# A forward and backward pass of four attention layers on one core: spread weight loads, halved score tiles, 66 identity products and a few moved steps

## The chip, the cores and the metric

The kernel runs on one core of one Trainium2 chip. The metric is the device time of one execution in microseconds (us). Three runs of the kernel before gave 2131.43, 2122.83 and 2129.14, so the median is 2129.14. Engines are named as in the profile: PE is TensorE (matrix products; PEld its weight loads), DVE is VectorE, ACT is ScalarE, POOL is GpSimd, and SP is SyncE, whose queue (SPq) issues every DMA of this kernel in program order.

## The reference

A sequence of 2048 rows of width 640 passes through four residual layers with two sets of weights, A, B, A, B. Each layer normalises its input, projects it to 32 heads of 20 columns, applies attention, projects back and adds the input. Layers 0 and 2 (A) are linear attention, layers 1 and 3 (B) are softmax attention in a window of 256 rows. The outputs are the last `x`, and the gradients for the input and the four weight matrices.

```python
def _A_ref(x, wqkv, wo):                     # H = 32, Dh = 20
    q, k, v = heads(x @ wqkv)
    phi = lambda t: jnp.where(t > 0, t + 1, jnp.exp(t)) + 1e-6
    pq, pk = phi(q), phi(k)
    kv, z = einsum("bhsd,bhse->bhde", pk, v), einsum("bhsd->bhd", pk)
    o = einsum("bhqd,bhde->bhqe", pq, kv) / (einsum("bhqd,bhd->bhq", pq, z)[..., None] + 1e-6)
    return merge(o) @ wo
def _B_ref(x, wqkv, wo):                     # causal, window W = 256
    p = softmax(where(mask, q @ k.T * Dh ** -0.5, -1e9))
    return merge(p @ v) @ wo
for f, w in ((_A_ref, A), (_B_ref, B), (_A_ref, A), (_B_ref, B)):
    x = x + f(_layernorm(x), *w)
out, vjp = jax.vjp(...);  grads = vjp(grad_out)
```

## The kernel before

The rows are cut into 16 tiles of 128. The kernel is one long program whose order on each engine is written by hand: every step of every tile is a closure with a place (a slot number), `forward` and `core` sort them by place, and the engines' queues are filled in that order. The table `PLACES` holds the offsets. Nothing reorders them afterwards; an engine does its own list in order and waits where an operand or a buffer is not ready. DMAs go to SP either at once (`dma`) or, through `put` (L153), so many slots later.

**The forward** has three overlapping stretches. `plan_first` (L650) does layer 0's projections, six slots per tile: products with `WA`, feature maps on ACT and DVE (L670 to L672), whose result tile `pqk` has two buffers and is stored to HBM by SP. The weights of layer 1, `WB`, are loaded in this stretch, at the places `ld` (L49, L365). From slot 118 on, `plan_front` (L523) finishes layer 0 for a tile and begins layer 1: quotients `o` on DVE (L559 to L561), transposes on PE with a copy back (`flip`, L220), products with `WoA` and `WB`, and two DMA transposes `T<-s` that bring queries and keys into the form the scores need. `plan_scores` (L445) computes the scores of a tile in six visits of four blocks: 16 products into one PSUM tile `sT` of four banks (one buffer, L462), one exponential of 128x2048 on ACT (L469), masks on POOL (L477, L480), and products with the values (`ops`, L286). Layers 2 and 3 repeat this from slot 302 on. `warm` (L233) issues products of the identity with itself into a PSUM tile from the ring `st.ps`; nobody reads them. The lists `fw` and `fn` (L64, L65) give places and counts of such products in the forward; all counts are 0.

**The backward** of a B layer is `core` (L1433): visits of eight blocks, three or four blocks in each of two halves. A visit computes scores `s` and, three visits later, `dp`; ACT makes `e` (L811), POOL masks it (L826, L830), DVE multiplies `ds` (L815), PE or a DMA transpose turns it into `dsT` (L818, L837), and three visits after that `acc` adds the gradients (L854). The operands of a quarter of a chunk, the slabs, are loaded by `core_loads` (L1392): `slabT` and `slabqT` for scores, `slabks` and `slabqs` (two buffers) for `acc`. `plan_before` (L909) prepares the next chunk: loads of `gb` and `ob` (one buffer), PE transposes of `gb`, products, and `fold` and `split` on POOL. The backward of an A layer is `plan_linear` (L1117); the last step of a tile, two additions of 128x640 (L1220, L1229), is on POOL, for the last tile of layer 2 on DVE. In `passes` (L1502) the first three visits of layer 1's core are issued at the offsets `B1_` (L77) among the last steps of layer 2's backward. The weight gradients `wg` come last.

Of the kernel before, what the change touches and what calls it, by code (L numbers as in the profile page):

```python
# [10 lines left out]
ACT = mybir.ActivationFunctionType  # L11
# [3 lines left out]
F32 = mybir.dt.float32  # L15
P = 128
D = 640
H = 32
DH = 20
HP = 32  # L20
T = 2048
TT = T // P
DT = D // P
SPM = (True, True, False, True, True, False)
G = H // 4
# [9 lines left out]
CW = D // 2  # L35
# [6 lines left out]
PLACES = dict(  # L42
    f1=[0.2, 1.1, 3.6, 8.1, 10.1, 11.8, 13.6, 14.1, 14.5, 14.6, 14.5, 16.1],
    f2=[-30.6, -24.5, -23.3, -20.4, -18.2, -17.7, -16.5, -14.9, -13.5, -7.7, -5.9, -5.8, -4.8, -3.3, -1.7, 10.6, 11.7, 12.6, 14.3, 16.6, 22.8, 23.8, 23.9, 25.1, 26.9, 26.7],
    f3=[-36, -31.4, -27.1, -25.2, -23.8, -23.8, -19.6, -17.6, -17.1, -14.1, -9.6, -8.1, -6.3, -5.3, -5, -4, -1.2, 11.7, 12.2, 13.7],
    s1=[0, 1.33, 2.67, 3.8, 5.83, 6.97, 1.4, 1.43, 2.77, 6, 6.63, 8.17, 2.7, 4.8, 5.7, 5.8, 7.4, 8.5, 9.6, 10],
    s3=[-0.3, 0.83, 2.77, 4, 5.43, 6.67, 0.2, 2.8, 4.67, 4.8, 5.58, 6.72, 3.9, 5.3, 6, 6.1, 7.2, 8.1, 9.7, 9.9],
    wt=[100, 101.9, 104, 104, 108, 110, 112.5, 115.2, 118, 118, 120.5, 122, 124, 126, 128.5, 279.3, 280.7, 280.7, 282, 282.8, 283.4, 283.7, 284.8, 285.9, 287.7, 288, 288.2, 288.2, 289.1, 291.6, 291.8, 292.5, 292.8, 293, 293, 293, 293.2, 295.1, 296.4, 296.4],
    ld=[39.8, 61, 63, 69.7, 82.8],  # L49
    sp=[2.6, 1.1, -2.9, -3.4, 0.6, -3.8, 0.1, 0.4, 2, 1.8, 1.1, 0.8, 3, 1, 0.9, 0.5, 1.3, 1.1, 1, 1, 1.5],  # L50
    ms=[1, -0.2, 20, 31.2, 39.5],
    bf=[1.6, 4.2, 7.7, 10, 17.8, 7.7, 9.2, 10, 14, 28.4],
# [8 lines left out]
    ws1=[8, 8, 8, 8, 8, 8, 8, 8, 8, 8, 8, 8],  # L61
    wp=[1.5, 3.5, 7.2, 9.2, 12, 15, 18, 21],
    wn=[0, 0, 0, 0, 0, 0, 0, 0],
    fw=[100, 120, 136, 268, 284, 298, 420, 428],  # L64
    fn=[0, 0, 0, 0, 0, 0, 0, 0],  # L65
    l2=[-10.1, -1.3, 0.6, 1.1, 1.9, 3, 4.6, 6.4, 7, 7.3, 5, 8, 8.3, 10.2, 11.6, 14, 15.2, 15.3, 16, 16.2, 18.7, -2.5, 3.9],
    n1=[9.7, 0.5, 3.3, 3.6, 5.3, 9, 3, 4.7, 5.4, 5.6, 24],
    th=[0, 2, 1, 4, 1, 0, 0, 0, 0, 3, 0, 1, 0, 0, 0, 4, 8, 5, 0, 1, 2, 2, 1, 1],
# [5 lines left out]


TAILV = (0, 0, 1, 2, 3, 4, 5)
B1_ = (4, 5, 6)  # L77
BEF, BEF1 = -26, 14


# [11 lines left out]
class Kern:  # L92
# [209 lines left out]
    def forward(self, st):  # L302
# [8 lines left out]
        nc = self.nc  # L311
# [21 lines left out]
        WA, WoB = vp.tile([P, DT, QT], BF, name="WA"), wo.tile([P, DT, D], BF, name="WoB")  # L333
        WB, WoA = wp.tile([P, DT, QT], BF, name="WB"), wp.tile([P, DT, D], BF, name="WoA")

        def cols(w, kind, c):
            self.dma(w[:, :, c * D:(c + 1) * D], self.W[kind][:, c * D:(c + 1) * D].rearrange("(k p) n -> p k n", p=P))

        def square(w, kind):
            self.dma(w, self.Wo[kind].rearrange("(k p) n -> p k n", p=P))  # L340
# [14 lines left out]
        plan = []  # L355
        for t in range(TT):
# [5 lines left out]
        plan += [(a, lambda c=c: cols(WA, "A", c)) for a, c in zip((0.5, 1.5, 2.5), (1, 2, 0))]  # L362
        plan += [(a + (1.2 * k if a > 1 else 0), lambda R=R, k=k: pads(R, k)) for a, R in zip(PLACES["ms"], st.ring) for k in range(5)]
        plan += [(0.2, lambda: self.warm(36, st.ps.tile([P, 8, P], BF, name="warm", tag="m")))]
        plan += list(zip(PLACES["ld"], (lambda: square(WoA, "A"), lambda: cols(WB, "B", 1), lambda: cols(WB, "B", 0),  # L365
                                        lambda: cols(WB, "B", 2), lambda: square(WoB, "B"))))

        plan += [(a, lambda n=n: self.warm(n, st.ps.tile([P, 8, P], BF, name="warm", tag="m"))) for a, n in zip(PLACES["fw"], PLACES["fn"]) if n]
        stage = {"j": -1}
# [17 lines left out]
        turns = [(w, d_, j, n - 1) for w, d_, n in ((WA, self.WT["A"], NF), (WoB, self.WoT["B"], DT), (WB, self.WT["B"], NF), (WoA, self.WoT["A"], DT)) for j in range(n)]  # L387
        plan += [(a, lambda x=x, i=i: turn(*x, i % 4 != 3)) for i, (a, x) in enumerate(zip(PLACES["wt"], turns))]

        def scores():  # L390
            first.close()
            st.ps = ps
            st.pSs = ExitStack()
            st.pS = self.pool(st.pSs, "pS", 1, bass.MemoryType.PSUM, "right")
        c1, c3 = 118, B1 + 144
        plan += [(c1, lambda: self.close_outer(self.mz[0], [m[0:KB, 0:3 * KA] for m in st.M])), (c1 + 9, lambda: self.turn_outer(st, self.mz[0], self.mzT[0])),
                 (B1 - 1, scores), (c3, lambda: (self.close_outer(self.mz[2]), self.counted(st.outs, 2 * TT))),
                 (c3 + 9, lambda: self.turn_outer(st, self.mz[2], self.mzT[2]))]

        class B3_:  # L400
# [44 lines left out]
    def plan_scores(self, st, l, t, X):  # L445
        nc = self.nc
        nb = min(t, 2) + 1
        k0 = t - nb + 1
        blocks = [(g, i) for g in range(G) for i in range(nb)]
        nv = len(blocks) // 4  # L450
        home = {}

        def ring(k):
            R = st.ring[k % len(st.ring)]
            assert R["of"] == (l, k)
            return R

        def visit(v):
            if v == 0:
                X[t]["ob"] = st.fa.tile([P, D], BF, name="ob")  # L460
            qT = ring(t)["T"]
            s = st.pS.tile([P, 4, 512], F32, name="sT")  # L462
            for j, (g, i) in enumerate(blocks[4 * v:4 * v + 4]):
                for hh in range(4):
                    r0 = HP * hh
                    self.mm(s[:, hh, j * P:(j + 1) * P], ring(k0 + i)["T"][r0:r0 + HP, 1, g, :], qT[r0:r0 + HP, 0, g, :],
                            True, True, (r0, 0))
            e = st.fpe.tile([P, 4, 4 * P], BF, name="eT", tag="e")
            nc.scalar.activation(e, s, ACT.Exp)  # L469
            for j, b in enumerate(blocks[4 * v:4 * v + 4]):  # L470
                home[b] = e[:, :, j * P:(j + 1) * P]

        def masks(v):
            for g, i in blocks[4 * v:4 * v + 4]:
                e = home[g, i]
                if i == nb - 1:
                    nc.gpsimd.affine_select(out=e, in_=e, compare_op=ALU.is_ge, fill=0.0, base=0,  # L477
                                            pattern=[[0, 4], [1, P]], channel_multiplier=-1)
                elif nb == 3 and i == 0:
                    nc.gpsimd.affine_select(out=e, in_=e, compare_op=ALU.is_ge, fill=0.0, base=-1,  # L480
                                            pattern=[[0, 4], [-1, P]], channel_multiplier=1)

        def values(g):
            X[t]["pv"] = g
            self.b_pv(st, l, t, g, [home[g, i] for i in range(nb)], nb, [ring(k0 + i) for i in range(nb)], X[t]["ob"])
        if nb < 3:
            pv = [g + 2.99 for g in range(G)]
            sc = [(G * v / nv, G * v / nv + 0.9) for v in range(nv)]
        else:
            a = PLACES["s1" if l == 1 else "s3"]  # L490
            sc, pv = list(zip(a[0:6], a[6:12])), a[12:20]
        plan = []
        for v in range(nv):
            plan += [(sc[v][0], lambda v=v: visit(v)), (sc[v][1], lambda v=v: masks(v))]
        return plan + [(pv[g], lambda g=g: values(g)) for g in range(G)]
# [270 lines left out]
        return ("FPA", "PFA", "PAF", "FAP", "AFP", "APF")[PLACES["fo"][n % 24] if 48 <= n < 192 else 0]  # L766

    V0 = 8
    WARM = (8, 5)
    TAIL = 5  # L770

# [345 lines left out]
    def plan_linear(self, st, lp, l, t, X, WT, g_out):  # L1117

        nc = self.nc
        eng = nc.vector if l == 2 and t == TT - 1 else nc.gpsimd  # L1120
        sv = self.sv[l]
        i = t % 2
        x = {}
# [268 lines left out]
    def core_loads(self, l, c, qr, B):  # L1392
        sv = self.sv[l]
        t0 = 2 * c
        w0 = max(t0 - 2, 0)
        S = {}
        if qr == 0 and c == 0:
            B.kept = []
        new = dict(c=c, qr=qr, T=B.keep.tile([P, 2, 2, 2, P], BF, name="slabT", bufs=7))
        old = B.kept[-4] if c else None  # L1400
        B.kept.append(new)

        def part(kind, dst, k, a, n):
            if k == "T":
                out, src = dst.rearrange("p a t g f -> p (a t g f)"), sv[k][c][:, qr, a:a + n].rearrange("p a t f -> p (a t f)")
            else:
                out, src = dst.rearrange("p a t g f -> p t a (g f)"), sv[k][t0:t0 + 2, :, a:a + n, qr * 2 * P:(qr + 1) * 2 * P].rearrange("t p a f -> p t a f")
            self.put(kind if c or qr else 0, out, src, now=c + qr == 0)
        q = B.slab.tile([P, 1, 2, 2, P], BF, name="slabqT", bufs=2)
        part(16, new["T"], "T", 1, 2)  # L1410
        part(17, q, "T", 0, 1)
        S["qT"] = q[:, 0]

        def late():
            new["s"] = B.keep.tile([P, 1, 2, 2, P], BF, name="slabks", bufs=6)
            q = B.slab.tile([P, 1, 2, 2, P], BF, name="slabqs", bufs=2)
            part(18, new["s"], "s", 1, 1)
            part(19, q, "s", 0, 1)
            S["qs"] = q[:, 0]
        S["late"] = late  # L1420

        def window(k, a):
            def at(kk, n):
                i = w0 + kk - t0
                return new[k][:, a, i:i + n] if i >= 0 else old[k][:, a, 2 + i:2 + i + n]
            return at
        S["kT"], S["vT"], S["ks"] = window("T", 0), window("T", 1), window("s", 0)
        for nm in ("ds", "dT"):
            S[nm] = [B.ring[(t0 + i) % 4][nm] for i in range(2)]
        S["ring"] = [(B.ring[(t0 + i) % 4], (l, t0 + i)) for i in range(2)]  # L1430
        return S

    def core(self, st, l, g_out, B, hooks):  # L1433
# [4 lines left out]
        plan = []  # L1438
        dq = {}
        for c in range(1, NC):  # L1440
            for a, *f in B.next if c == 1 else self.plan_before(st, l, c, B):
                if c == 1:
                    a = self.V0 / 0.75 + a * (1 - self.V0 / 24) if a < 32 else a
                plan.append((32 * (c - 1) + a, *f))
# [286 lines left out]
```

## Time and profile before

| | us |
|---|---|
| median of three runs | 2129.14 |
| lowest and highest | 2122.83, 2131.43 |
| the profiled execution | 2130.39 |
| its span, first to last instruction | 2128.6 |
| DVE busy in it | 1387.4 |
| ACT busy in it | 1301.5 |
| POOL busy in it | 1014.2 |

The profile is of one execution, and all rows quoted here are from it. A row of the timeline has the start, the duration, the engine, the source line, the tiles (output, then inputs) and the count of merged instructions; in brackets behind it stands how long the engine sat idle before, and what ended that. A row of the table by windows has the stretch, its length, then for PE, PEld, DVE, ACT and POOL the busy time with the number of instructions, the granted clock of PE (1.00 is full speed), the share of the DMA engines and GB/s. The row of a group has the busy time, the mean duration in ns, and the idle time before with its releasers.

### The profile page before, as it was taken

The numbers are of one execution on the slowest core, as the hardware profiler recorded it, in microseconds if no ns is written. First come the engines' busy times: TensorE is split into PE (matmuls) and PEld (weight loads), VectorE is DVE, ScalarE is ACT, GpSimd is POOL, SyncE is SP. The second block draws the span as 40 slices with busy tenths as digits, with TensorE's granted clock in tenths as the row PEclk, the third lists the DMA queues.
The fourth block names the chain that finished last, engine by engine and source line by source line (L and its number), as shares of the span: only waits on it lengthen the run. The fifth ranks groups of instructions, "written<-read, shape, count | busy, mean of one in ns | idle before, by whom it ended". The sixth has DMA issues, their size and how long they took to land. (4 is left out here: it accounts for less than half of the span.)

```text
span 2128.6 us, 75619 instructions
## 1 busy us (share of the span) xinstructions
PE 1993.5 (94%) x32332; PEld 1533.7 (72%) x32332; DVE 1387.4 (65%) x2696; ACT 1301.5 (61%) x1818; POOL 1014.2 (48%) x1594
## 2 busy tenths in 40 slices
PE   8989999899988899999989988999998899999999
PEld 6667776667766777777758767777777788887644
DVE  7778886788865878788858868888886243310000
ACT  6558888468876777777747677777776244420000
POOL 1046666056666567777643356777774312220000
PEclk9999999999999999999999999999999999999999
DMA  7588876598884579889898836899887989979650
GB/s 255 200 213 227 225 212 189 186 234 219 217 218 125 157 164 188 183 188 188 176 281 251 229 112 127 180 193 191 196 175 206 308 241 271 277 199 308 221 169 19
DMA packets 667937, 432.17 MB, mean 203 GB/s; under 512 B 396880, under 2 KB 637904, under 8 KB 667344
## 3 DMA queue, kind: packets, MB, share of 16 engines
q1 hardware_dynamic: 667600, 427.34, 78.4%
q8 instruction: 252, 4.13, 0.8%
q14 instruction: 85, 0.70, 0.1%
HBM read 197.79 MB, written 147.32 MB: 162 GB/s over the span
## 5 line engine op out<-in xcount | busy, mean ns | idle before, releaser
L815 DVE TENSOR_TENSOR ds<-dp,e 128x1024 bf16<-128x1024 f32 (+1 forms) x368 | 441.5, 1200 | 121.4 <-PE s L204 76.5
L811 ACT ACTIVATE e<-s 128x1024 bf16<-128x1024 f32 (+1 forms) x368 | 371.7, 1010 | 116.4 <-PE s L204 78.7
L469 ACT ACTIVATE eT<-sT 128x2048 bf16<-128x2048 f32 x180 | 338.3, 1879 | 96.9 <-PE sT L204 73.5
L204 PE MATMUL wg<-rhs,lhs 128*128 128x240 bf16 (+3 forms) x2720 | 370.2, 292 | 0.9 <-DMA lhs<-o 0.9
L204 PEld LDWEIGHTS <-lhs 128*128 128x128 bf16 x2720 | 250.9, 98 | 93.5 <-DMA lhs<-o 1.1
L830 POOL TENSOR_SCALAR_AFFINE_SELECT e<-e 128x256 bf16<-128x256 bf16 x448 | 182.8, 422 | 130.9 <-ACT e L811 130.9
L477 POOL TENSOR_SCALAR_AFFINE_SELECT eT<-eT 128x512 bf16<-128x512 bf16 x256 | 163.7, 643 | 114.5 <-ACT eT L469 110.4
L204 PEld LDWEIGHTS <-dqT 128*128 128x128 bf16 x1920 | 174.0, 98 | 59.6 <-issue 5.4
L826 POOL TENSOR_SCALAR_AFFINE_SELECT e<-e 128x512 bf16<-128x512 bf16 x256 | 162.8, 636 | 91.2 <-ACT e L811 89.8
L204 PE MATMUL acc<-slabqs,ds 128*128 128x20 bf16 x2880 | 193.6, 172 | 2.8 <-ACT part L896 2.2
L204 PE MATMUL acc<-ds,e 128*128 128x20 bf16 x2880 | 191.0, 172 | 0.0
L204 PEld LDWEIGHTS <-ds 128*128 128x128 bf16 x2880 | 171.4, 96 | 22.4 <-issue 18.0
L204 PE MATMUL dp<-slabT,dT 32*128 32x128 bf16 (+1 forms) x1920 | 149.1, 248 | 38.4 <-DVE ds L815 34.1
L1355 DVE CAST wr<-wg 128x240 bf16<-128x240 f32 (+3 forms) x48 | 22.8, 474 | 230.9 <-PE wg L204 214.4
L204 PEld LDWEIGHTS <-e 128*128 128x128 bf16 x2880 | 163.5, 96 | 5.2 <-issue 2.4
L204 PE MATMUL dense<-WB,hnT 128*128 128x320 bf16 x960 | 162.1, 303 | 1.3 <-ACT hnT L228 0.7
L204 PE MATMUL dense<-WTA,dqT 128*128 128x320 bf16 x960 | 156.0, 299 | 0.8 <-ACT dh L1208 0.4
L204 PE MATMUL dense<-WTB,dqT 128*128 128x320 bf16 x960 | 153.4, 301 | 0.0
L1353 ACT CAST wr<-wg 128x240 bf16<-128x240 f32 (+3 forms) x32 | 13.2, 412 | 227.7 <-PE wg L204 208.9
L1220 POOL TENSOR_TENSOR dh<-dh,lg 128x640 f32<-128x640 f32 x31 | 44.6, 1439 | 225.6 <-DVE s L1217 225.6
L204 PE MATMUL s<-slabT,slabqT 32*128 32x128 bf16 (+1 forms) x1920 | 147.4, 249 | 4.2 <-DMA slabqT<-T 1.9
L480 POOL TENSOR_SCALAR_AFFINE_SELECT eT<-eT 128x512 bf16<-128x512 bf16 x224 | 143.3, 640 | 15.0 <-ACT eT L469 13.6
(189 smaller groups left out, 4393.3 us busy)
## 6 DMA issues: line engine op xcount, KB each, us to landing
T<-T SPq DMA_DIRECT2D x96, 256.0 KB, 3.8
s<-s SPq DMA_DIRECT2D x32, 512.0 KB, 3.3
slabT<-T SPq DMA_DIRECT2D x64, 256.0 KB, 3.7
dqkv<-dqa SPq DMA_DIRECT2D x32, 480.0 KB, 4.4
rhs<-dqkv SPq DMA_DIRECT2D x32, 480.0 KB, 6.3
rhs<-dqkv SPq DMA_DIRECT2D x16, 960.0 KB, 6.7
hn<-hn SPq DMA_DIRECT2D x64, 160.0 KB, 3.1
lpqk<-pqk SPq DMA_DIRECT2D x16, 640.0 KB, 6.4
```

Of the source, the lines that this page charges most:

```text
L204: return self.nc.tensor.matmul(out, lhsT=lhsT, rhs=rhs, start=start, stop=stop, skip_group_check=True, **kw)
L469: nc.scalar.activation(e, s, ACT.Exp)
L477: nc.gpsimd.affine_select(out=e, in_=e, compare_op=ALU.is_ge, fill=0.0, base=0, pattern=[[0, 4], [1, P]], channel_multiplier=-1)
L480: nc.gpsimd.affine_select(out=e, in_=e, compare_op=ALU.is_ge, fill=0.0, base=-1, pattern=[[0, 4], [-1, P]], channel_multiplier=1)
L811: nc.scalar.activation(u.e[:, :, 0:w], s[:, :, 0:w], ACT.Exp)
L815: nc.vector.tensor_tensor(out=d.ds[:, :, 0:w], in0=d.dp[:, :, 0:w], in1=d.e[:, :, 0:w], op=ALU.mult)
L826: nc.gpsimd.affine_select(out=v, in_=v, pattern=[[0, 4], [1 if far else -1, P]], **kw)
L830: nc.gpsimd.affine_select(out=v, in_=v, pattern=[[0, 2], [1 if far else -1, P]], **kw)
L1220: eng.tensor_tensor(out=x["dh"], in0=x["dh"], in1=L["g"][:, i, :], op=ALU.add)
L1353: nc.scalar.copy(o[:, 0:w], ps[:, 0:w])
L1355: nc.vector.tensor_copy(o[:, 0:w], ps[:, 0:w])
```

## The change

Seven edits. (1) `WB` is loaded in six pieces of 320 columns at slots 47 to 67 in place of three of 640 at 61 to 69.7. (2) Identity products are issued in the forward: 24 at slot 127.795, 28 at 145.996, 14 at 147.995. On PE's list these stand ahead of the transposes `flip<-o` of the second tile, of a group `sT`, and of the next group `sT`. (3) For the last four tiles of layer 3 the pool of `sT` is opened anew, with two buffers of two banks; a visit is two halves of eight products, each with an exponential of 128x1024. (4) The two additions of the last tile of layer 2's backward are on POOL. (5) `B1_` is one slot later: on PE, five products `dense<-WTA,dqT` go ahead of the core's first scores, and the others of that tile ahead of the second and third. (6) In chunk 0 the load of `slabqs` is put off by 2.1 slots, so on SP it stands behind the next quarter's `slabqT` and `slabT` and the load of `WTB`. (7) From chunk 2 on `gb` and `ob` are loaded four slots earlier; on SP they go past up to two DMA transposes `dsT`.

```diff
-    ld=[39.8, 61, 63, 69.7, 82.8],
+    ld=[39.8, 47, 51, 55, 59, 63, 67, 82.8],
...
-    fw=[100, 120, 136, 268, 284, 298, 420, 428],
-    fn=[0, 0, 0, 0, 0, 0, 0, 0],
+    fw=[127.795, 145.996, 147.995],
+    fn=[24, 28, 14],
...
-B1_ = (4, 5, 6)
+B1_ = (5, 6, 7)
...
-        def cols(w, kind, c):
-            self.dma(w[:, :, c * D:(c + 1) * D], self.W[kind][:, c * D:(c + 1) * D].rearrange("(k p) n -> p k n", p=P))
+        def cols(w, kind, c, n=D):
+            self.dma(w[:, :, c * n:(c + 1) * n], self.W[kind][:, c * n:(c + 1) * n].rearrange("(k p) n -> p k n", p=P))
...
-        plan += list(zip(PLACES["ld"], (lambda: square(WoA, "A"), lambda: cols(WB, "B", 1), lambda: cols(WB, "B", 0),
-                                        lambda: cols(WB, "B", 2), lambda: square(WoB, "B"))))
+        plan += list(zip(PLACES["ld"], (lambda: square(WoA, "A"), *(lambda c=c: cols(WB, "B", c, CW) for c in range(6)), lambda: square(WoB, "B"))))
...
-        def scores():
+        def scores(first=first):
             first.close()
             st.ps = ps
-            st.pSs = ExitStack()
+            st.pSs = first = ExitStack()
             st.pS = self.pool(st.pSs, "pS", 1, bass.MemoryType.PSUM, "right")
...
-                 (B1 - 1, scores), (c3, ...
+                 (B1 - 1, scores), (B3 + G * self.HALVES - 0.35, lambda: scores(st.pSs)), (c3, ...
...
-            s = st.pS.tile([P, 4, 512], F32, name="sT")
-            for j, (g, i) in enumerate(blocks[4 * v:4 * v + 4]):
-                for hh in range(4):
-                    r0 = HP * hh
-                    self.mm(s[:, hh, j * P:(j + 1) * P], ...)
             e = st.fpe.tile([P, 4, 4 * P], BF, name="eT", tag="e")
-            nc.scalar.activation(e, s, ACT.Exp)
+            m = 2 if l == 3 and t >= self.HALVES else 4
+            for h in range(0, 4, m):
+                s = st.pS.tile([P, m, 512], F32, name="sT", bufs=4 // m)
+                for j, (g, i) in enumerate(blocks[4 * v:4 * v + 4]):
+                    for hh in range(h, h + m):
+                        r0 = HP * hh
+                        self.mm(s[:, hh - h, j * P:(j + 1) * P], ...)
+                nc.scalar.activation(e[:, h:h + m], s, ACT.Exp)
...
+    HALVES = 12
...
-        eng = nc.vector if l == 2 and t == TT - 1 else nc.gpsimd
+        eng = nc.gpsimd
...
-            self.put(kind if c or qr else 0, out, src, now=c + qr == 0)
+            self.put(kind if c or qr else 0, out, src, now=c + qr == 0, delay=delay)
...
-            part(19, q, "s", 0, 1)
+            part(19, q, "s", 0, 1, 2.1 if c == 0 and qr else None)
...
-            for a, *f in B.next if c == 1 else self.plan_before(st, l, c, B):
+            for a, *f in B.next if c == 1 else self.plan_before(st, l, c, B, None, -4):
```

More of the change, by code (lines that the diff above doesn't have):

```diff
@@ L396, in forward @@
         plan += [(c1, lambda: self.close_outer(self.mz[0], [m[0:KB, 0:3 * KA] for m in st.M])), (c1 + 9, lambda: self.turn_outer(st, self.mz[0], self.mzT[0])),
-                 (B1 - 1, scores), (c3, lambda: (self.close_outer(self.mz[2]), self.counted(st.outs, 2 * TT))),
+                 (B1 - 1, scores), (B3 + G * self.HALVES - 0.35, lambda: scores(st.pSs)), (c3, lambda: (self.close_outer(self.mz[2]), self.counted(st.outs, 2 * TT))),
                  (c3 + 9, lambda: self.turn_outer(st, self.mz[2], self.mzT[2]))]
@@ L461, in visit @@
             qT = ring(t)["T"]
-            s = st.pS.tile([P, 4, 512], F32, name="sT")
-            for j, (g, i) in enumerate(blocks[4 * v:4 * v + 4]):
-                for hh in range(4):
-                    r0 = HP * hh
-                    self.mm(s[:, hh, j * P:(j + 1) * P], ring(k0 + i)["T"][r0:r0 + HP, 1, g, :], qT[r0:r0 + HP, 0, g, :],
-                            True, True, (r0, 0))
-            e = st.fpe.tile([P, 4, 4 * P], BF, name="eT", tag="e")
-            nc.scalar.activation(e, s, ACT.Exp)
+            e = st.fpe.tile([P, 4, 4 * P], BF, name="eT", tag="e")
+            m = 2 if l == 3 and t >= self.HALVES else 4
[4 more added lines that the diff above has]
+                        r0 = HP * hh
+                        self.mm(s[:, hh - h, j * P:(j + 1) * P], ring(k0 + i)["T"][r0:r0 + HP, 1, g, :], qT[r0:r0 + HP, 0, g, :],
+                                True, True, (r0, 0))
+                nc.scalar.activation(e[:, h:h + m], s, ACT.Exp)
             for j, b in enumerate(blocks[4 * v:4 * v + 4]):
@@ L1401, in core_loads, with part @@
         B.kept.append(new)
-        def part(kind, dst, k, a, n):
+        def part(kind, dst, k, a, n, delay=None):
             if k == "T":
```

## The prediction

> **What bounds the kernel now.** I read the page's busy shares first, then the chain that ended last, then the granted clock in windows of 3.41 us, and last the waits of PE. The shares and the chain:
>
> ```profile
> span 2128.6 us, 75619 instructions
> PE 1993.5 (94%) x32332; PEld 1533.7 (72%) x32332; DVE 1387.4 (65%) x2696; ACT 1301.5 (61%) x1818; POOL 1014.2 (48%) x1594
> PE 22%; DMA 1%; DVE 1%; issue 0%; ACT 0%; SPq 0%; POOL 0%; POOLq 0%; DVEq 0%; ACTq 0%
> core 0: 2128.6 us, clock 0.985
> ```
>
> PE is busy for 94% of the span, and the part of the chain that could be followed back (a quarter of the span) is PE. So time is to be won only where PE stands still (135 us in all) or where it runs slowly. The slow part is in the last row: where the clock is not 1.00 it is 0.50, so a mean of 0.985 is 0.015 x 2128.6 / 0.5 = 64 us at half speed, some 19 windows of 3.41 us. A window of that kind with the one ahead of it, a window of transposes alone, and the first work of the program (these rows are of tables by window and of the timeline):
>
> ```profile
> 96.83:100.24 3.41, 1.80 (x28) 1.34 (x26) 3.12 (x11) 1.95 (x3) 0.55 (x1) 1.00 0.57 197
> 100.24:103.66 3.42, 3.42 (x20) 2.16 (x19) 1.36 (x3) 1.38 (x2) 0.00 (x0) 0.50 0.13 48
> ...
> 1076.46:1079.87 3.41, 2.17 (x30) 0.71 (x2) 1.49 (x2) 1.00 1.12 406
> ...
> 1.55 3.66 PE L236 MATMUL warm<-ident 128*128 128x128 bf16 x36 [1.55 <-POOL ident masks.py:199]
> 5.66 0.45 PE L225 MATMUL flip<-ident,hn 128*128 128x128 bf16 x5 [0.46 <-DVE hn L518]
> ```
>
> In the first row PE was busy for 1.80 us of 3.41, and in the next window the clock was 0.50 although PE never paused. So a wait of PE costs twice: the wait, and half speed in the window behind it, which is worth at most 3.41 / 2 = 1.7 us when PE is busy throughout. The third row (the tile `flip` alone) keeps 1.00 with 2.17 us of transposes.
>
> **The change part by part.** The seven edits stand on stretches that follow one another on PE, so their gains are added. I work against the profiled execution, 2130.39 (span 2128.6 and 1.8 around it); the median of the runs is 1.25 below that.
>
> *Spread loads of `WB`.* One view is the timeline about 51 us, the other the DMA groups (KB each, us to landing):
>
> ```profile
> 43.44 0.39 SPq L148 DMA_DIRECT2D pqk<-pqk  x1
> 50.88 0.49 DVE L672 SCALAR_TENSOR_TENSOR pqk<-dense,e 128x320 bf16<-128x320 f32 x1 [2.77 <-DMA pqk<-pqk]
> 51.42 0.84 PE L204 MATMUL dense<-WA,h2T 128*128 128x320 bf16 x5 [2.15 <-DVE pqk L672]
> ...
> 52.46:55.87 3.41, 3.41 (x16) 2.09 (x17) 1.93 (x7) 0.89 (x3) 0.55 (x1) 0.50 0.53 185
> ...
> WB<-in_B_wqkv_dram SPq DMA_DIRECT2D x3, 800.0 KB, 8.1
> pqk<-pqk SPq DMA_DIRECT2D x16, 320.0 KB, 3.0
> ```
>
> DVE waits 2.77 us for a buffer of `pqk`, whose store was issued at 43.44 behind two loads of `WB` and took over 7 us where the median is 3.0. PE waits 2.15 for DVE and then has a full window at half clock. With pieces of half the size, begun 14 slots earlier, two pieces' bytes no longer stand ahead of that store at once; at its median it lands 4 us ahead of the need. Gain 2.15 + 1.7 = 3.8, bounds 0 and 3.9. The six issues add three to SP, which is not late here.
>
> *The 66 products.* Their price, and the three instructions that they go ahead of:
>
> ```profile
> 75.39 0.44 PE L378 MATMUL flip<-ident,WA 128*128 128x128 bf16 x5
> 76.35 0.72 PE L378 MATMUL flip<-ident,WA 128*128 128x128 bf16 x10
> 99.74 0.34 PE L225 MATMUL flip<-ident,o 128*128 128x128 bf16 x3 [1.59 <-DVE o L561]
> 102.22 0.49 DVE L576 TENSOR_TENSOR xm<-dense,xi 128x320 bf16<-128x320 f32 x1 [1.61 <-PE dense L204]
> 126.27 0.24 PE L204 MATMUL sT<-T,T 32*128 32x128 bf16 x4 [1.97 <-DMA T<-s]
> 128.69 0.30 PE L204 MATMUL sT<-T,T 32*128 32x128 bf16 x4 [0.88 <-ACT eT L469]
> ...
> 127.55:130.96 3.41, 2.53 (x33) 1.64 (x30) 2.74 (x8) 2.65 (x2) 1.31 (x2) 0.50 0.97 304
> ...
> 131.35 1.22 POOL L477 TENSOR_SCALAR_AFFINE_SELECT eT<-eT 128x512 bf16<-128x512 bf16 x2 [1.33 <-ACT eT L469]
> ```
>
> One more product of 128x128 costs (0.72 - 0.44) / 5 = 0.056. So 24, 28 and 14 take 1.34, 1.57 and 0.78, and the waits are 1.59, 1.97 and 0.88: each lot fits. The wait of 1.59 lies in the window that begins at 96.83; with 1.34 more PE is busy for 3.1 of 3.41 there, and I expect the clock to stay. Behind it DVE waits 1.61 for products at half clock: of 1.7 I take 1.4. The second half-clock stretch reaches from 127.55 into the masks at 131.35; doubling PE's speed would take 1.3 off its 2.53 busy and 1.7 off the next window, 3.0 in all, but masks on POOL stand between (1.33 idle for ACT, then 1.22), so I take half, 1.4. Together 2.8; bounds 4.7 (1.7 + 3.0), and a loss of 66 x 0.056 = 3.7 if the waits that cover them have gone elsewhere: the waits shift as the spread loads move this stretch by 4 us.
>
> The Trainium skill, "TensorE: Matmul & The Clock Gate", Part 1 "What's actually happening", has a free-running window of 3413 ns and full clock only after activity; the windows above agree. Its Part 4, "PE-mode transpose", holds that transposes do not count as PE being busy for the clock; these 66 products are issued as transposes, so by it their gain would be 0 and the sum 2.8 worse. The rows of 1076.46 and 5.66 speak against it here.
>
> *Halved score tiles.* A group of the page (mean ns), and the timeline of the last tiles:
>
> ```profile
> L811 ACT ACTIVATE e<-s 128x1024 bf16<-128x1024 f32 x336 | 345.6, 1029 | 97.9 <-PE s L204 60.2 <-POOL e L830 17.2 <-POOL e L826 13.5
> ...
> 600.94 0.29 PE L204 MATMUL sT<-T,T 32*128 32x128 bf16 x8
> 618.92 1.88 ACT L469 ACTIVATE eT<-sT 128x2048 bf16<-128x2048 f32 x1 [0.58 <-PE sT L204]
> 648.97 0.24 PE L204 MATMUL sT<-T,T 32*128 32x128 bf16 x4 [0.42 <-ACT eT L469]
> 658.00 0.85 PE L204 MATMUL dense<-WoB,obT 128*128 128x320 bf16 x5 [2.10 <-DVE obT L230]
> ```
>
> From 600.94 to 648.97 are 19 visits: 2.53 each, of which row 618.92 shows 1.88 of exponential and 0.58 in which ACT waits for the 16 products, since there is one buffer. With two, ACT goes from half to half: 2 x 1.029 = 2.06. ACT has other work and PE has visits that need more, so I take the middle, 2.3, which is 19 x 0.23 = 4.4, less about 1 for the last tile, whose end waits for DVE (2.10). Gain 3.3. Bounds: 19 x 0.47 = 8.9, and a loss of 1, where a quarter of the 24 visits pays the 0.18 by which two exponentials are longer than one. That is 24 x 0.18 = 4.3 us more on ACT, hidden in its idle 0.58 per visit.
>
> *Order of DMAs in the backward.* Waits of PE (us in total, times, longest) and one row:
>
> ```profile
> 691.19 0.23 PE L204 MATMUL s<-slabT,slabqT 32*128 32x128 bf16 x2 [0.65 <-DMA slabT<-T]
> ...
> PE flip L225 <- DMA gb<-in_grad_out_dram: 2.3, 4, 1.3
> PE acc L204 <- DMA dsT<-ds: 4.4, 4, 1.8
> ```
>
> `slabqs` put off: the operands that the scores wait for go ahead of it, so at most 0.65; I take 0.4 (a loss only if `acc` were then short of it; it comes three visits behind `dp`, so bound it at the longest DMA wait here, 1.8). `gb` and `ob` four slots earlier: at most the 2.3, I take 1.2. They go ahead of `dsT` transposes in each of six chunks per layer, twelve in all, and `acc` stands behind these; the loss is the rival below.
>
> *The last tile of layer 2 and `B1_`.*
>
> ```profile
> 1233.70 0.34 PE L204 MATMUL s<-slabT,slabqT 32*128 32x128 bf16 x4 [1.90 <-DMA slabqT<-T]
> 1240.24 1.12 DVE L1220 TENSOR_TENSOR dh<-dh,lg 128x640 f32<-128x640 f32 x1
> 1241.46 0.82 DVE L1229 TENSOR_TENSOR gn<-dh,lna 128x640 bf16<-128x640 f32 x1
> 1243.21 0.23 PE L204 MATMUL dp<-slabT,dT 32*128 32x128 bf16 x2 [3.30 <-DVE ds L815]
> ...
> 1243.71:1247.12 3.41, 3.41 (x30) 2.24 (x29) 1.90 (x3) 0.81 (x1) 3.18 (x4) 0.50 0.16 53
> ...
> L1220 POOL TENSOR_TENSOR dh<-dh,lg 128x640 f32<-128x640 f32 x31 | 44.6, 1439 | 225.6 <-DVE s L1217 225.6
> L1229 POOL TENSOR_TENSOR lgn<-dh,lna 128x640 bf16<-128x640 f32 x30 | 46.1, 1538 | 19.4 <-ACT lna L1228 9.0 <-issue 5.6 <-POOL dh L1220 4.3
> 1252.90 1.22 POOL L826 TENSOR_SCALAR_AFFINE_SELECT e<-e 128x512 bf16<-128x512 bf16 x2
> 1254.66 0.96 DVE L815 TENSOR_TENSOR ds<-dp,e 128x768 bf16<-128x768 f32 x1 [0.67 <-PE s L204]
> ```
>
> `dp` waits 3.30 for the first `ds` on DVE, which stands behind the two additions (1.12 + 0.82 = 1.94); the next window is at half clock. Off DVE, `ds` comes up to 1.94 earlier; the five products ahead of the first scores (0.84 for such a five, above) fill part of the 1.90. At most 1.94 + 0.84 + 1.7 = 4.5. But POOL gets 1.44 + 1.54 = 3.0 more, ahead of its fold and of the masks at 1252.90, and a `ds` on DVE follows these at 1254.66. So about 3.0 of the 4.5; bounds 4.5 and a loss of 3.0 - 1.94 = 1.1.
>
> *Sum.* 3.8 + 2.8 + 3.3 + 0.4 + 1.2 + 3.0 = 14.5. 2130.4 - 14.5 = 2115.9; I say 2116.
>
> **The rivals.**
>
> *Given back.* The first two terms (6.6) rest on waits with a plain cause. The other four (7.9) hand work to ACT, POOL and an earlier place on SP, and each may meet the next wait: `obT` on DVE in layer 3, the masks on POOL in layer 1. If a quarter of them is left, the time is 2130.4 - 6.6 - 2.0 = 2121.8. For it: POOL works 3.18 of 3.41 us in the window of 1243.71. Against it: the waits of 0.58 recur visit by visit.
>
> *The store stays late.* If DMA traffic as a whole, not the two large loads, holds the store of `pqk`, the 3.8 is missing: 2119.7. Against it: the median of 3.0.
>
> *Transposes do not hold the clock.* The products fill waits but the windows behind stay at 0.50: 2118.7. The Trainium skill's Part 4 named above says so. The rows of the clock speak against it: only transposes ran from 1.55 to 5.66, 36 in 3.66 us, or 0.10 each, and the five at 5.66 take 0.45, as at 75.39 at full clock.
>
> *Slower: `dsT` late.* 640 KB of `gb` and `ob` now stand ahead of one or two `dsT` transposes in twelve chunks, and `acc` waits. At the longest wait that such a transpose causes now, 1.8, that is 21.6 in place of the 1.2 won: 2130.4 - 13.3 + 21.6 = 2138.7. It makes the kernel slower from 13.3 / 12 = 1.1 us per chunk, slower by over 0.5% from 2.0. Against it: only four waits of this kind in the whole run, 4.4 us.
>
> **How the numbers follow.** A measurement of this kernel can tell about 0.5% from no change: below 2118.5 is faster, above 2139.8 slower. Chances: the forecast 0.55 (own range 2107 to 2121, since halving and the last tile reach 7 us further down, and terms fall short by 5), given back 0.26, the store 0.07, the clock 0.04, `dsT` late 0.08. Of the forecast 0.5 lies below 2118.5, of the rest of the first three rivals 0.09: faster 0.59. Slower by over 0.5% are some two thirds of the last rival, 0.05. Same 0.36. There is one more spread: an edit shifts all that follows against fixed windows of 3.41 us, so any of the 17 or so untouched half-clock windows may go or a new one come, 1.7 at most each; two or three of them make 3 to 5 us either way. The range is 2107 to 2125: up it takes in given back and this spread, and leaves out the last rival and some of the rest.
>
> **What would show it.** Right: no wait for `pqk` near 51, and a clock of 1.00 in the window behind; the clock at 1.00 behind the first 24 and the 28 products; ACT with two exponentials of about 1.03 per visit in the last tiles of layer 3, without idle time for `sT`; no `dp` wait of 3.3 at the turn to layer 1's backward. Wrong: half-clock windows behind the products (then transposes do not count); `L477` or `L1229` as the wait that ends last; waits of `acc` for `dsT` well over 4.4 us in sum (then the fourth rival).

## The result, and the profile after

The changed kernel takes 2119.64 us (median of 15 runs, 2117.04 to 2124.0), the kernel before 2127.96 (15 runs, 2122.83 to 2143.9). The ratio is 0.9964 with a 95% interval of 0.9952 to 0.9977: 7.7 us faster by this ratio, 0.36% (the two medians differ by 8.3). I had forecast 2116 and a gain of 14.5; the way and the range were right, the gain about half.

The page of the profile after, its span and busy times, and the mean clock of the core; the execution profiled took 2119.64:

```profile
span 2117.9 us, 75800 instructions
PE 1996.9 (94%) x32398; PEld 1537.9 (73%) x32398; DVE 1385.5 (65%) x2694; ACT 1302.3 (61%) x1842; POOL 1019.6 (48%) x1596
core 0: 2117.9 us, clock 0.987
```

PE still bounds it. It is busy for 3.4 us more than before (66 products, and the halved tiles, below), and yet the span is 10.7 shorter, so PE stands still for 14.1 us less; the mean clock is 0.987 where it was 0.985. To see where, I matched the two traces: the same instruction of DVE in both, its start in each, and the difference. The last column is the kernel with `gb` and `ob` at their old place, which is told of below (E10).

```
what has just been passed            before    after   lead      E10    lead
WB loaded (L672 waited at 50.88)       61.0     57.2    3.8     57.4     3.6
the 66 products                       142.6    135.1    7.4    136.2     6.4
tile 12 of layer 3 begins             600.7    593.8    6.9    594.2     6.5
last tile of layer 3                  669.4    661.3    8.1    660.8     8.6
chunks 0 and 1 of layer 3's core      713.9    703.9   10.0    703.8    10.1
end of layer 3's core                1058.8   1047.5   11.4   1044.0    14.9
before the turn to layer 1's core    1226.1   1214.7   11.3   1212.4    13.7
behind the turn                      1260.3   1244.4   15.8   1242.0    18.3
chunk 1 of layer 1's core            1302.8   1285.3   17.5   1282.8    19.9
chunk 4                              1439.8   1426.8   13.1   1422.0    17.8
chunk 5 or 6                         1544.7   1532.6   12.0   1527.2    17.5
last products of the gradients       2125.4   2114.5   10.8   2108.3    17.1
```

The lead grows where the spread loads, the products and the turn stand, by 1.2 over layer 3's halved tiles (600.7 to 669.4) and by 1.9 in the first two chunks of its core, and between 1303 and 1545 it shrinks by 5.5. The rows that answer to those of before, first the two waits for products (timeline) and the windows about the first and the second lot:

```profile
94.08 1.50 PE L236 MATMUL warm<-ident 128*128 128x128 bf16 x24
95.93 0.34 PE L225 MATMUL flip<-ident,o 128*128 128x128 bf16 x3 [0.25 <-DVE o L562]
...
119.28 1.72 PE L236 MATMUL warm<-ident 128*128 128x128 bf16 x28
121.42 0.24 PE L204 MATMUL sT<-T,T 32*128 32x128 bf16 x4 [0.42 <-DMA T<-s]
...
93.02:96.43 3.41, 3.14 (x52) 2.68 (x50) 3.12 (x11) 1.95 (x3) 0.55 (x1) 1.00 0.58 199
96.43:99.85 3.42, 3.14 (x31) 2.17 (x29) 2.37 (x6) 1.39 (x2) 0.00 (x0) 1.00 0.24 88
...
120.33:123.74 3.41, 2.99 (x58) 2.50 (x56) 1.02 (x4) 1.82 (x1) 0.00 (x0) 1.00 1.06 292
123.74:127.16 3.42, 3.32 (x54) 2.66 (x54) 2.97 (x7) 2.52 (x3) 2.17 (x4) 1.00 1.00 272
```

The waits of 1.59 and 1.97 have become products with 0.25 and 0.42 behind them, and the windows that follow are at 1.00 where they were at 0.50. The clock is 1.00 from 14.2 to 355.5 us of this profile; the profile before had four windows at 0.50 there, one at 52.46, one at 100.24 and two from 127.55. The waits of PE after the change (in us, times, longest), those that the prediction spoke of:

```profile
PE sT L204 <- ACT eT L470: 8.1, 17, 1.3
PE acc L204 <- DMA dsT<-ds: 7.6, 11, 1.7
PE dense L204 <- DVE obT L230: 2.8, 2, 2.5
PE s L204 <- DMA slabqT<-T: 0.6, 1, 0.6
...
PE dense L204 <- DVE pqk L673: 0.7, 2, 0.5
```

The wait of 2.15 for `pqk` is gone. `acc` waits for `dsT` eleven times where it was four, 7.6 in place of 4.4; no wait of `flip` for `gb` is left.

### The profile page after: what moved, and what is told of

Same layout as the page of the kernel before. It is cut to its first block, busy times and chain, and to the rows that moved or that the text cites. A ratio compares the mean times of both kernels' runs of the same rounds, so it can differ in the third digit from the quotient of the medians.

```text
span 2117.9 us, 75800 instructions
## 1 busy us (share of the span) xinstructions
PE 1996.9 (94%) x32398; PEld 1537.9 (73%) x32398; DVE 1385.5 (65%) x2694; ACT 1302.3 (61%) x1842; POOL 1019.6 (48%) x1596
## 5 line engine op out<-in xcount | busy, mean ns | idle before, releaser
L470 ACT ACTIVATE eT<-sT 128x2048 bf16<-128x2048 f32 (+1 forms) x204 | 339.1, 1679 | 93.8 <-PE sT L204 76.6
L1355 ACT CAST wr<-wg 128x240 bf16<-128x240 f32 (+3 forms) x32 | 13.2, 413 | 228.4 <-PE wg L204 222.3
L481 POOL TENSOR_SCALAR_AFFINE_SELECT eT<-eT 128x512 bf16<-128x512 bf16 x224 | 144.4, 644 | 14.4 <-ACT eT L470 13.2
```

Of the source, the lines that this page charges most:

```text
L470: nc.scalar.activation(e[:, h:h + m], s, ACT.Exp)
L1355: nc.scalar.copy(o[:, 0:w], ps[:, 0:w])
```

## The experiments

Theory: six of the seven edits do nearly what was forecast, with halving worth less than forecast because PE pays for it, and the seventh, the early loads of `gb` and `ob`, costs instead of paying, since the `dsT` transposes behind them on SP's queue come late. Rivals: the products do nothing (transposes leave the clock alone), each gain is taken back by a later wait, or the lead is lost to half-clock windows that fall by chance. Executions scatter much: 35 of the kernel before on one chip took 2116.12 to 2133.16. So each edit is read twice, by the ratio with its interval, and by the place in the trace at which the lead changes. Microseconds given with a ratio are worked out from the ratio; the medians alone differ from them by up to 2.5 us. One execution of each version was profiled.

**The early loads.** E3 is the changed kernel without them, E8 the kernel before with them alone.

```diff
(e3_late_gb, from the kernel after)
-            for a, *f in B.next if c == 1 else self.plan_before(st, l, c, B, None, -4):
+            for a, *f in B.next if c == 1 else self.plan_before(st, l, c, B):
(e8_early_gb_only, from the kernel before: the same line the other way)
```

> The changed kernel with gb and ob loaded at their old place. Theory 1 (the earlier loads push dsT transposes back): acc waits for dsT fall from 7.6 us in sum to 4 to 5, flip waits for gb come back at 2 to 3 us, the time stays within 1.5 us of 2119.6. Rival (the earlier loads are worth what was forecast, and late dsT transposes are chance): +1.2 or more, and the waits of acc for dsT stay near 7.6.

> The kernel before with gb and ob loaded four slots earlier and nothing else. Theory 1 (the earlier loads cost, since dsT transposes behind them come late): 3 to 6 us longer than before, 1.0014 to 1.0028 of it, with acc waiting 7 to 9 us in sum for dsT, and flip no more for gb. Rival (they pay 1.2 as forecast, and are bad only together with the other edits): 0.9994.

E3: 2114.18 us, 0.9938 (0.9919 to 0.9956). E8: 2127.66, 1.0030 (1.0017 to 1.0042). Taking the loads back gains 0.0026, adding them alone costs 0.0030: about 6 us either way (by the medians alone 2.4 and 4.2), which is more than both theories had expected for E3. The waits of PE, first E3, then E8:

```profile
PE acc L204 <- DMA dsT<-ds: 1.0, 1, 1.0
PE flip L225 <- DMA gb<-in_grad_out_dram: 0.3, 1, 0.3
```

```profile
PE acc L204 <- DMA dsT<-ds: 6.7, 11, 1.7
```

In E8, as in the kernel after, eleven waits for `dsT`; in E3 one. E3's profile is a good one: E10, the same program once more, has five, 3.6 us in sum. Over all fourteen profiles of this document the six with early loads have 9 to 14 such waits, the eight without them 1 to 6; the sums overlap (5.0 to 10.3 us with, 1.0 to 8.8 without). The place is seen on SP's queue. The kernel after, in layer 1's core (SP's own issues, then PE):

```profile
1398.64 1.24 SPq L148 DMA_TRANSPOSE dsT<-ds  x1
1399.92 0.58 SPq L148 DMA_DIRECT2D gb<-g  x1
1400.60 0.42 SPq L148 DMA_DIRECT2D ob<-o  x1
1401.06 3.46 SPq L148 DMA_TRANSPOSE dsT<-ds  x2
...
1407.92 0.36 PE L204 MATMUL acc<-slabks,dsT 128*128 128x20 bf16 x8 [1.42 <-DMA dsT<-ds]
```

The two loads are issued just ahead of two transposes; the products that need the first start at 1407.92, 6.9 us after its issue, and PE has stood for 1.42. The transposes that stand directly behind an `ob` land in a median of 5.2 us in the kernel after (10 of them, up to 6.8) and are used 4.4 to 6.9 after issue; for five of the ten PE has to wait. In E3 they are others, land in 3.8 (8 of them), are used 6.1 after issue, and PE waits for none (counted over the issues in the two traces). E3's issues in a chunk of layer 3's core:

```profile
887.02 5.87 SPq L148 DMA_TRANSPOSE dsT<-ds  x3
892.95 0.57 SPq L148 DMA_DIRECT2D gb<-in_grad_out_dram  x1
893.61 0.42 SPq L148 DMA_DIRECT2D ob<-o  x1
895.27 1.23 SPq L148 DMA_TRANSPOSE dsT<-ds  x1
```

Three transposes go ahead of the loads and the next is issued 1.2 us behind them. Against the rival: the waits did not stay near 7.6. And the gain of 1.2 for `gb`, which was the reason for the edit in my sum, was not there to be had: E3 loads `gb` at the old place and PE waits 0.3 for it, where the one profile of before showed 2.3. More than half of that 2.3 is one wait of 1.3 at 702.7, which is gone in E3 and E10 without the early loads: the sixth edit is enough to take it, as the account of `slabqs` below shows.

**The products.** E1 is the changed kernel without them, E7 the kernel before with them alone, E9 is E3 without them.

```diff
(e1_no_products and e9_late_gb_no_products)
-    fn=[24, 28, 14],
+    fn=[0, 0, 0],
(e7_products_only, from the kernel before)
+    fw=[127.795, 145.996, 147.995],
+    fn=[24, 28, 14],
```

> The changed kernel without the 66 products. Theory 1 (products fill the waits and so keep the clock): the first shifted stretch of the trace lost 3.6 us here, so about 2123, with half-clock windows back behind the flip<-o and sT waits of the forward. Rival (transposes leave the clock as it is, and the windows stayed at full clock by chance of their phase): no difference, 2119 to 2120.

> The kernel before with the 66 products alone. Theory 1: in the trace some 3 us are won between 96 and 135 us, and nothing else is done; the waits of flip for gb and of acc for dsT in the backward stay at about 2 to 3 and 4 to 6 us if they belong to the kernel, and move freely if they are chance of one execution. Time against before: -3, so 0.9986 of it. Rival (products do nothing for the clock): 1.000, and the windows behind the waits are at half clock as before.

> The changed kernel with the loads of gb and ob at their old place and without the 66 products: what the products are worth where the dsT waits no longer scatter the time. Theory 1 (3.3 us, as the traces lie at 134 us): 2117.5 where late gb alone gave 2114.2. Rival (their gain is taken back by later waits, as without them the changed kernel took the same time): 2114 to 2115.

E1: 2118.03 us, 0.9962 (0.9946 to 0.9979). E7: 2123.5, 1.0000 (0.9985 to 1.0016). E9: 2117.09, 0.9971 (0.9956 to 0.9985), where E3 had 0.9938. At their place the traces agree: E1 falls 3.3 us behind the kernel after by 134 us, E9 3.9 behind E3, and E7 gains 4.1 on the kernel before between 100 and 133. The windows of E1 at the place quoted above:

```profile
93.02:96.43 3.41, 1.68 (x22) 1.05 (x19) 3.09 (x10) 1.94 (x4) 0.55 (x1) 1.00 0.48 158
96.43:99.84 3.41, 3.41 (x18) 2.33 (x19) 0.99 (x2) 1.29 (x2) 0.00 (x0) 0.50 0.10 35
123.74:127.15 3.41, 2.72 (x25) 1.56 (x25) 2.61 (x7) 2.52 (x2) 1.37 (x3) 0.50 0.96 282
127.15:130.57 3.42, 3.42 (x31) 2.60 (x30) 1.08 (x3) 0.69 (x1) 1.16 (x2) 0.50 0.46 154
```

The same window with 1.68 us of work in place of 3.14 is followed by one at 0.50. The second stretch agrees. So do the other profiles: the four without the products (before, E8, E1, E9) all have a half-clock window that begins between 96 and 101 and two from 123 to 128, and none of the ten with them has one that begins between 94 and 131. So the rival that transposes leave the clock alone has fallen. In the total the answers differ: nothing in E1 and E7, 0.0033 (7 us) in E9. Each has some 0.002 of uncertainty, so 3 to 4 us at the end are not shown, nor excluded. In E7 the backward is that of before, instruction for instruction, and yet its lead went from 2.4 us at 714 to 7.4 at 1059 and 5.0 at 1226. Waits for DMAs and half-clock windows move by that much from one execution to the next:

```profile
PE acc L204 <- DMA dsT<-ds: 3.5, 5, 1.4
PE flip L225 <- DMA gb<-in_grad_out_dram: 1.0, 2, 0.7
```

(E7's waits; before's profile had 4.4 and 2.3 with the same instructions.)

**The halved score tiles.** E2 is the changed kernel with whole tiles, E13 is E3 with whole tiles. E5 has whole tiles whose products are issued in the order of the halves.

```diff
(e2_whole_tiles, e13_late_gb_whole_tiles)
-            m = 2 if l == 3 and t >= self.HALVES else 4
+            m = 4
(e5_two_heads, from the kernel after)
+            s = st.pS.tile([P, 4, 512], F32, name="sT")
             for h in range(0, 4, m):
-                s = st.pS.tile([P, m, 512], F32, name="sT", bufs=4 // m)
                 for j, (g, i) in enumerate(blocks[4 * v:4 * v + 4]):
                     for hh in range(h, h + m):
                         r0 = HP * hh
-                        self.mm(s[:, hh - h, j * P:(j + 1) * P], ...)
-                nc.scalar.activation(e[:, h:h + m], s, ACT.Exp)
+                        self.mm(s[:, hh, j * P:(j + 1) * P], ...)
+            nc.scalar.activation(e, s, ACT.Exp)
```

> The changed kernel with whole score tiles (16 products, one exponential of 128x2048) in layer 3's last four tiles. Theory 1 (with two heads at a time in place of four the score products take PE twice as long, some 0.22 us per visit, so what ACT wins is lost on PE): about +1, 2120 to 2121, with PE's waits for ACT back at some 9 us between 590 and 660 and PE's busy time there some 5 us less. Rival (halving is worth what was forecast, and the trace hid it behind half-clock windows): +3.3, about 2123.

> That base with whole score tiles in layer 3. Theory 1 (ACT's gain is PE's loss): within 1 us of the base in the stretch to 660, and within 0.0005 of it in all. Rival (halving is worth the 3.3 forecast): base + 0.0016.

> The changed kernel with one whole score tile and one exponential per visit in layer 3's last four tiles, but its 16 products issued two heads at a time, as the halves do it. Theory 1 (with two heads at a time the products take PE twice as long): in the trace 16 products span about 0.66 us from first to last end against 0.44 with four heads at a time, and the stretch from 590 to 660 is about 5 us longer than with whole tiles in the old order. Rival (the order of the products costs nothing, PE is held up elsewhere): the stretch takes as long as with whole tiles, within 1 us.

E2: 2119.01 us, 0.9968 (0.9955 to 0.9981). E13: 2117.78, 0.9948 (0.9925 to 0.9970), its base below 0.9941. Halving is worth 0.0004 and 0.0007 of before, 1 to 1.5 us. By the traces E13 loses 1.1 to its base over the four tiles (from 600 to 669), E2 1.3 to the kernel after; the means over all profiles, below, say 2.0. The same 60 us in E2 and in the kernel after:

```profile
594.00:654.00 60.00, 48.86 (x1000) 38.03 (x998) 32.30 (x77) 45.32 (x27) 39.54 (x69) 0.97 0.78 202
```

```profile
594.00:654.00 60.00, 53.21 (x1011) 39.94 (x1011) 33.51 (x78) 46.15 (x50) 39.99 (x68) 0.97 0.82 203
```

PE's work in instructions is nearly the same, but it is busy for 4.4 us more with the halves. The waits for ACT that halving removed (from 13.2 in E2 to 8.1, 5.1 us) came back for the most part as busy time. Nor was ACT freed of its waits: from 594 to 669 it stands idle for `sT` for 11.0 us with the halves, for 13.8 in E2. One visit in E2, and one in the kernel after:

```profile
610.72 0.24 PE L204 MATMUL sT<-T,T 32*128 32x128 bf16 x4 [0.98 <-ACT eT L470]
610.78 0.24 PE L204 MATMUL sT<-T 32*128 32x128 bf16 x4
610.83 0.29 PE L204 MATMUL sT<-T,T 32*128 32x128 bf16 x8
```

```profile
610.82 0.23 PE L204 MATMUL sT<-T,T 32*128 32x128 bf16 x2
610.87 0.23 PE L204 MATMUL sT<-T 32*128 32x128 bf16 x2
610.93 0.29 PE L204 MATMUL sT<-T,T 32*128 32x128 bf16 x4
611.73 0.23 PE L204 MATMUL sT<-T,T 32*128 32x128 bf16 x2 [0.52 <-ACT eT L470]
611.78 0.23 PE L204 MATMUL sT<-T 32*128 32x128 bf16 x2
611.84 0.29 PE L204 MATMUL sT<-T,T 32*128 32x128 bf16 x4
```

Products on different groups of 32 rows run at the same time: four of them every 0.055 us with whole tiles, two of them every 0.055 with halves. So from its first start to its last end a half takes 0.40 (610.82 to 611.22), as long as a whole tile (610.72 to 611.12), and a visit has two, with PE at a stop between them. E5 refutes the simpler reading that I had put down, that the order of two heads at a time is slow in itself:

```profile
609.82 0.26 PE L204 MATMUL sT<-T,T 32*128 32x128 bf16 x4 [1.01 <-ACT eT L470]
609.88 0.26 PE L204 MATMUL sT<-T 32*128 32x128 bf16 x4
609.93 0.32 PE L204 MATMUL sT<-T,T 32*128 32x128 bf16 x8
```

All 16 begin within 0.22 us again (0.19 in E2) and the stretch is 1.1 us longer than E2's, not 5: with nothing between them the two halves overlap. E5's time, 2121.44 or 0.9989 (0.9972 to 1.0006), is longer for another reason: it has the early loads, and `acc` waits 10.3 us for `dsT` in its profile against 8.4 in E2's; that may be 1.9 of some 4.5 us, the rest is open. That two lots of products standing apart eat up ACT's gain is what the three traces agree on; no run takes it away by itself. Halves by blocks, which would keep four heads side by side, were not tried.

**The version without the early loads, and two edits taken from it.** E10 is E3 once more; E11 and E12 undo one edit of it.

```diff
(e10_late_gb_again: e3_late_gb unchanged)
(e11_late_gb_old_turn)
-B1_ = (5, 6, 7)
+B1_ = (4, 5, 6)
-        eng = nc.gpsimd
+        eng = nc.vector if l == 2 and t == TT - 1 else nc.gpsimd
(e12_late_gb_old_loads)
-    ld=[39.8, 47, 51, 55, 59, 63, 67, 82.8],
+    ld=[39.8, 61, 63, 69.7, 82.8],
(and the three loads of 640 columns as before)
```

> The changed kernel with gb and ob at their old place once more, as the base of the next three and as the version that may beat both kernels. Theory 1: 0.992 to 0.9955 of before (0.9938 the first time). Rival (the first time was luck of few executions): 0.9964, as the changed kernel.

> That base with the last tile's two additions on DVE and B1_ at (4, 5, 6). Theory 1 (the 4.2 us that the trace shows at the turn reach the end): base + 0.002 of before. Rival (they are taken back by later waits): within 0.0005 of the base.

> That base with the three large loads of WB. Theory 1 (2.15 us of wait and 1.7 of half clock come back near 51): 3.8 us at that place in the trace, base + 0.0018 of before. Rival (DMA traffic as a whole held the store; the piece size matters little): the wait for pqk stays away, and the time is the base's.

E10: 2115.35 us, 0.9941 (0.9916 to 0.9965), so the first result holds: this version is 0.6% faster than the kernel before, 12.5 us by the ratio (11.3 by the medians, with 2126.62 for before). By both of its runs it beats the changed kernel too, though the intervals overlap. E11: 2120.48, 0.9963 (0.9944 to 0.9983): the turn is worth 0.0022 or 4.7 us. E12: 2119.14, 0.9960 (0.9937 to 0.9982): the spread loads are worth 0.0019 or 4.0 us. The intervals overlap, but the places in the traces say the same: E12 falls 2.6 us behind E10 between 33 and 67 us, E11 3.7 between 1206 and 1240. So the rival that DMA traffic as a whole held the store has fallen, though smaller pieces and the earlier start were not tried apart; that later waits take the gains back has nothing for it in these two runs. E12's waits for `pqk`:

```profile
PE dense L204 <- DVE pqk L674: 3.2, 4, 2.1
```

The wait of 2.1 is back, but in this profile no half-clock window stands behind it (1.00 from 43.9 to 57.5), and so 2.6 and not 3.8 is lost there. The other three profiles with the large loads (before, E7, E8) have one that begins between 52 and 54.

**The turn in the changed kernel.** The same undoing with the early loads still in.

```diff
(e4_old_turn, from the kernel after: the two edits of e11)
```

> The changed kernel with the last tile's two additions on DVE and B1_ at (4, 5, 6) as before. Theory 1 (the turn to layer 1's backward gave 4.8 us, as the two traces lie): about 2124.4, with a dp wait of about 3.3 us near 1230. Rival (POOL gives a third back, as was forecast): +3.0, about 2122.6.

E4: 2119.07 us, 0.9968 (0.9956 to 0.9980), only 0.0004 above the changed kernel, so both expectations missed. At the place it is 4.2 us behind (from 2.4 ahead at 1202 to 1.9 behind at 1236), with the wait back:

```profile
1228.92 0.23 PE L204 MATMUL dp<-slabT,dT 32*128 32x128 bf16 x2 [3.31 <-DVE ds L817]
```

By the end it has regained them: from 1303 to 1640, in layer 1's core, it takes 338.8 us where the kernel after takes 341.5 (times of before). Its waits for `dsT` explain 0.7 of that (2.4 in sum against 3.1, from 1260 to 1660). Whether the early loads always take that much of the turn's gain, or the profile after fell badly there, stays open.

## Why the prediction was right, and where it was wrong

The fourteen profiles can be set side by side: for each edit the stretch in which it works, from one DVE instruction to another (named by their starts in the profile before), in every profile without the edit and in every one with it. The profiles differ in other edits too, but at another place.

| edit | stretch | us without it | us with it | means apart | forecast |
|---|---|---|---|---|---|
| spread loads | 33 to 61 | 26.5 to 28.7 (4 profiles) | 24.0 to 24.2 (10) | 3.8 | 3.8 |
| products | 61 to 142.6 | 81.6 to 82.1 (4) | 77.4 to 78.8 (10) | 3.8 | 2.8 |
| halved tiles | 600.7 to 669.4 | 67.5 to 69.3 (6) | 65.9 to 67.5 (8) | 2.0 | 3.3 |
| `slabqs` | 685.7 to 705.9 | 19.2 to 21.1 (3) | 18.0 to 18.2 (11) | 2.2 | 0.4 |
| the turn | 1226.1 to 1302.8 | 75.7 to 76.8 (5) | 70.5 to 70.7 (9) | 5.5 | 3.0 |
| early loads | 713.9 to 1058.8 and 1302.8 to 1640 | 675.3 to 684.6 (8) | 680.4 to 686.5 (6) | -4.6 | 1.2 |

- **Spread loads** (3.8): right. 3.8 in the trace by 61 us and in the means, 4.0 by the ratio of E12 to E10.
- **Products** (2.8): right in its mechanism, each lot fits its wait and the window behind stays at 1.00. At the place 3.6 in the pair of profiles, 3.8 in the means. In the total not settled (0, 0 and 7 us). One of the two rows on which I rested it was weak: at the start of the program the clock rose behind 36 transposes in the profile before, but in the profile after it rose only at 10.8, and the five there still took 0.71:

```profile
5.68 0.71 PE L225 MATMUL flip<-ident,hn 128*128 128x128 bf16 x5
```

- **Halved tiles** (3.3): too much, 1 to 2 us against 3.3. The failed step is "with two, ACT goes from half to half": I let PE's products cost what they had, 16 as one lot. PE's wait for ACT fell by 5.1, but two lots apart kept it busy 4.4 longer. The last tile's wait for `obT`, which I took off as 1, grew from 2.1 to 2.5.
- **`slabqs`** (0.4): too little; 2.2 in the means (1.2 to 3.1). The edit was not tried by itself, but of the seven it is the only one that the eleven shorter profiles share and the three longer lack. The wait of 0.65 for `slabT` at 691 is gone, and with it the one of 1.3 for `gb` at 702.7, which I had booked under the next edit. In the profile before, `slabT` and `gb` stood behind `slabqs` on SP's queue, and from 680 to 712 that queue waited 17.9 us for `acc`. In E3, whose loads of `gb` are at their old place, `slabT` goes ahead of `slabqs`, and `gb` is issued 5.9 us ahead of its use; before it was issued 4.7 us ahead of the time at which PE came to it. First before, then E3:

```profile
694.42 0.37 SPq L148 DMA_DIRECT2D slabqs<-s  x1
695.75 0.43 SPq L148 DMA_DIRECT2D slabT<-T  x1
696.70 0.43 SPq L148 DMA_DIRECT2D gb<-in_grad_out_dram  x1
...
680.05 0.43 SPq L148 DMA_DIRECT2D slabT<-T  x1
684.20 0.37 SPq L148 DMA_DIRECT2D slabqs<-s  x1
685.12 0.43 SPq L148 DMA_DIRECT2D gb<-in_grad_out_dram  x1
```

- **Early `gb` and `ob`** (1.2 won): the wrong sign; this is the step that failed most. It cost 5.5 (E3) to 6.4 us (E8) by the ratios, 2.4 and 4.2 by the medians, 4.6 in the means of the table. I had priced the gain from one profile's 2.3 us of waits, of which 1.3 go with the sixth edit as well, and which another execution of the same backward shows as 1.0 (E7), and had put the loss, correctly described, into the fourth rival with a chance of 0.08. Its price there, 1.8 for each of twelve chunks, was too high: 0.2 to 0.5 per chunk.
- **The turn** (3.0): too little; 3.7 to 4.6 in the pairs of traces, which end before 1303, 5.5 in the means up to there, 4.7 by E11. The wait for `slabqT`, of whose 1.90 I counted 0.84, fell to 0.6. The loss to POOL that I took off did not come; the masks on POOL kept up, and `dp` waits 0.97 where it waited 3.30:

```profile
1226.64 1.40 POOL L1222 TENSOR_TENSOR dh<-dh,lg 128x640 f32<-128x640 f32 x1 [0.94 <-DVE s L1219]
...
1228.60 1.54 POOL L1231 TENSOR_TENSOR gn<-dh,lna 128x640 bf16<-128x640 f32 x1
...
1227.14 0.23 PE L204 MATMUL dp<-slabT,dT 32*128 32x128 bf16 x2 [0.97 <-DVE ds L935]
```

The sum without the early loads was 13.3; E10 measures 12.5 and E3 13.2 (11.3 and 10.7 by the medians), each with an interval of 4 to 5 us to either side. So the seventh edit, 1.2 not won and 2 to 6 lost, is half or more of what was missing from 14.5. That the rest comes out so close is in part luck. At their places the other five gains add up to 17.3, 4 more than forecast, since `slabqs`, the turn and the products gave more than halving fell short by; and 4 to 7 of the 17.3 do not reach the end. So the rival "given back" is not refuted. One place is known: from 1303 to 1640 the six profiles without early loads but with other edits take 336.9 to 341.1, before and E7 take 336.4 and 335.4. Which edit does that is not shown.

## What to carry to other kernels

A load that is moved up a queue is paid by what it goes past: price the transfers behind it by how little time they have to spare, before pricing the wait that it removes. A tile halved so that one engine need not wait can take the other engine as long per half as the whole did, if what ran side by side is then split. Where executions differ by more than an edit is worth, take the size at the edit's place from matched traces, and the sign at the end from undoing it in the final version.

## What was not expected of the hardware

In the window of 93.02 the clock of the next one hangs on the products: with 1.68 us of PE's work it fell to 0.50, and with 1.50 us of identity products more, issued as transposes, it stayed. That is no threshold in busy time: in the profile before the window that begins at 1230.03 has 1.53 us of PE's work and the next is at 1.00, the one at 1585.03 has 2.82 and the next is at 0.50. What decides between these two is not shown. The Trainium skill, "TensorE: Matmul & The Clock Gate", Part 4 "PE-mode transpose", does not let transposes count for the clock; the windows with and without the products say that here they do.

The score products run four at a time, every 0.055 us, as long as four groups of rows are issued close together, and it makes little difference whether the order is all four heads or two at a time (0.19 against 0.22 us for 16); a stop between the pairs does. And 35 executions of one program on one chip spread over 17 us (0.8%), and E7's backward shows the same instructions gaining and losing up to 5 us in waits for DMAs and in half-clock windows.
